# Starting the row maxima ten blocks ahead and the attention four slots earlier

## The chip, the cores and the metric

The kernel runs on one core of one Trainium2 chip. Its engines are TensorE (PE in the profile; its weight loads are PEld), VectorE (DVE), ScalarE (ACT), GpSimd (POOL) and SyncE (SP), which here only issues DMAs. The metric is the device time of one execution in microseconds.

## The reference

One sequence of 2048 tokens of width 512, in float32. Biases, layer norm parameters and a batch do not occur.

```python
xn = layernorm(x)
# attention on layernormed tokens: 32 heads of 16, a window of 256 keys, causal
q, k, v = split(xn @ wqkv)
mask = (i - j >= 0) & (i - j < 256)
s = softmax(where(mask, q @ k.T * 16**-0.5, -1e9)) @ v @ wo
# channel MLP of the normalised tokens, normalised once more, 512 -> 1792 -> 512
g = silu(gelu(layernorm(xn) @ w1 + b1) @ w2 + b2)
out = x + s * g
```

Products are made to float32 precision with three passes of a shorter type: every operand is held as a high part and a low remainder, and high x high, high x low and low x high are summed.

## The kernel before, in words

There are three stages. A prologue normalises x, transposes it into `big` (the array called xnT in the profile, high and low part, four chunks of 512 tokens) and makes the first projections. The attention works on eight quads of four heads in 128 slots (`t` from 0 to 127, sixteen to a quad, one block of 128 keys each). The MLP and the output follow. The change touches the first two.

**Slots.** One loop, `for t in range(-16, end + 1)`, writes out the program in order, and each engine keeps that order; so does SP from the loads on. A slot with t >= 0 does, in this order on PE: `prob_block` for the second half of the heads (scores of one key block against up to 384 queries, into the tile `stb`; ACT takes the exponent to `pt`; POOL blanks the two edge squares), `max_block`, the first half of the slot's fills, `prob_block` for the other half of the heads, the second half of the fills, and `pv_step` for the block before (the product with the values, `zo<-pt,vt`, copied to `oraw`). Negative slots hold fills and, from t = -12, maxima.

**Maxima ahead.** `max_block(n, qb)` for block m = 16 n + qb runs in slot m - `LEAD`, with LEAD = 12: eight score matmuls (into `xy` and `zo`; four in the first two blocks of a quad), then on DVE a predicated copy that masks, and a reduction. After four blocks `max_rows` splits and transposes the maxima on DVE; one slot later SP writes them to DRAM (`mT_d`), and at the end of the slot after that it reads them back as rows of `slots[n % 2]` (the tile `qk`). There they stand as an extra row beside the queries, so that the score matmul subtracts the maximum itself; a matching row of the keys holds ones. A block of scores in slot kb reads queries up to kb + 2.

**The row of ones.** `slots` has two tiles of 128 x 8192. In tile 0 all is cleared at the start by three engines (`clear_rows`). Tile 1 shares its memory with `x23`, the last two chunks of x, and is opened at t = -5; `clear_part` then fills it on ACT in four pieces of 128 x 2048, in slots -4 to -1.

**Fills.** `fills[t, half]` holds matmuls of other work. In the prologue `group(c)` gives four slots per chunk c, from t = 4 c - 16: the Q/K projection of quad 0 (`job_qk(0, c)`, 12 matmuls of 128 x 512), two value jobs (`job_v`, 24 matmuls of 128 x 256 for two blocks of tokens), and the transposes of the next chunk (`job_x`, 16). The projections of quad 1's chunks 0 and 1 (`job_qk(1, 0)` and `(1, 1)`) lie over t = -2 to 2. All other projections are written with `tandem`: two chunks at a time, as matmuls of half the array's height, 48 of them over four to six slots. A projection ends with a copy by ACT (the high part, `sh`), a subtraction that leaves the remainder (`pjr`; by DVE for quad 0, by POOL for the others) and six DMAs into the slot tile: four with the high part, two with the remainder. In `pair_qk` the slot of the POOL subtraction is set by `quiet`, which takes the next free slot whose number leaves 1 or 2 when divided by four.

**PSUM.** `xy`, `zo` and the two banks `fb` are there throughout. Before t = 0 a pool `ps_st` of two more banks serves value jobs and transposes; it closes at t = 0 and its banks become `stb`.

**Layer norm of x.** `lns` says after which slot the last two chunks are normalised: each pair of tiles takes statistics on DVE, a power on POOL, a shift on DVE and the application on ACT.

In the last slots, where no maxima are left, `prob_block` uses `xy` as a second score tile:

```python
both = xy if p and 16 * n + kb + LEAD >= 16 * NQ else stb[0]
```

Of the kernel before, what the change touches and what calls it, by code (L numbers as in the profile page):

```python
# [18 lines left out]
P = 128  # L19
# [4 lines left out]
NQ = H // 4  # L24
EPS = 1e-5
NEG = -3.0e38
LEAD = 12
EARLY = 10


# [19 lines left out]
def mixer_kernel(ctx, tc, x, wqk, wv, wo, w1, b1, w2, b2, out):  # L50
# [96 lines left out]
    def open_slot(i):  # L147
# [9 lines left out]
    w_d = {"w1": dram.tile([P, NF * 512], F32, name="w1_d"), "w2": dram.tile([P, NF * 512], F32, name="w2_d"),  # L157
           "wo": dram.tile([P, 4 * 512], F32, name="wo_d")}
    g_d = dram.tile([NF, P, 512], F32, name="g_d")
    mT_d = dram.tile([NQ, NCH, 32, P], F32, name="mT_d")  # L160


# [10 lines left out]
    def fill_bank():  # L173

        turn[0] ^= 1
        return fb[turn[0]]
# [3 lines left out]
    def clear_rows(i, parts):  # L180

        flat = slots[i].rearrange("p q l t -> p (q l t)")
        ones = upper.unsqueeze(1)
        for eng, lo, hi in parts:
            if eng is nc.scalar:
                eng.copy(flat[:, lo: hi].rearrange("p (k t) -> p k t", t=P), ones.to_broadcast([P, (hi - lo) // P, P]))
            else:
                eng.memset(flat[:, lo: hi].bitcast(F32), float(lo >= 4096))

    def clear_part(k):  # L190
        flat = slots[1].rearrange("p q l t -> p (q l t)")[:, 2048 * k: 2048 * (k + 1)]
        nc.scalar.activation(flat, vt[:, 0, 0, DH: DH + 1].to_broadcast([P, 2048]), AF.Identity, scale=float(k >= 2))

    ident = const.tile([P, P], F32, name="ident")
    upper = const.tile([P, P], F32, name="upper")
    mhalf = const.tile([P, 4], F32, name="mhalf")
# [5 lines left out]
    nc.gpsimd.memset(mhalf, -0.5)  # L202
    make_identity(nc, ident)
    clear_rows(0, ((nc.vector, 0, 2048), (nc.scalar, 4096, 7168), (nc.gpsimd, 2048, 4096), (nc.gpsimd, 7168, 8192)))
    nc.vector.memset(negc, NEG)
    mask = upper.bitcast(I32).unsqueeze(1).unsqueeze(1).to_broadcast([P, 2, 2, P])
    neg = negc.unsqueeze(2).unsqueeze(2).to_broadcast([P, 2, 2, P])
# [106 lines left out]
    def job_v(hf, i):  # L314

        box = []

        def mm(k):
            if k == 0:
                box.append(ps_st.tile([P, 2, 256], F32, tag="b", name=f"pv_{hf}_{i}"))  # L320
            j, kt, (a, b) = k // 12, k % 12 // 3, PASSES[k % 3]
            kb = 2 * i + j
            nc.tensor.matmul(box[0][:, j], big[:, a, kt, P * kb: P * (kb + 1)], wva[:, b, kt],
                             start=(k % 12 == 0), stop=(k % 12 == 11))

        def finish():
            nc.scalar.copy(vt[:, 2 * i: 2 * i + 2, :, 0:DH], box[0].rearrange("p b (h d) -> p b h d", d=DH))
        return [(109, mm, k) for k in range(24)], finish
# [277 lines left out]
    def at(t, fn, *args):  # L606
        plan.setdefault(t, []).append((fn, args))
# [3 lines left out]
    def behind(t, fn, *args):  # L611

        ends.setdefault(t, []).append((fn, args))
# [41 lines left out]
    nc.gpsimd.affine_select(out=upper, in_=upper, pattern=[[1, P]], compare_op=ALU.is_gt,  # L655
                            fill=0.0, base=0, channel_multiplier=-1)
    for i in range(8):
        behind(-14 + i // 4, nc.sync.dma_start, xn_d[i], xs[i // 4][i % 4])

    def group(c):  # L660
        if c == 0:
            (ops, finish), (x_ops, _) = job_v(0, 1), job_x(1)
            return [job_qk(0, 0), job_v(0, 0), (ops[:12] + x_ops, lambda: None), (ops[12:], finish)]
        return [job_qk(0, c), job_v(0, 2 * c), *([job_x(c + 1)] if c + 1 < NCH else []), job_v(0, 2 * c + 1)]
    groups = [(4 * c - 16, 4, group(c)) for c in range(NCH)]
    for t0, n, jobs in groups:
        fills.update(spread(jobs, [(t0 + i // 2, i % 2) for i in range(2 * n)]))

    for place, todo in spread([job_qk(1, 0), job_qk(1, 1)], [(t, k) for t in range(-2, 3) for k in range(2)]).items():
        fills.setdefault(place, []).extend(todo)  # L670
    soon = {}
    tandem(3, 8, pair_qk(1, 2), pair_qk(1, 3))
    for n, spans in enumerate((((9, 14), (15, 19)), ((20, 24), (25, 30)), ((31, 35), (36, 41)), ((42, 47), (48, 53, 51)),
                               ((75, 79), (80, 84)), ((85, 90), (93, 98))), 2):
        for c, span in zip((0, 2), spans):
            tandem(*span[:2], pair_qk(n, c), pair_qk(n, c + 1), *span[2:])
    for i, (t0, t1) in enumerate(((54, 58), (59, 63), (64, 68), (69, 74))):
        tandem(t0, t1, pair_v(2 * i), pair_v(2 * i + 1))
    for f, *span in ((6, 99, 104, 102), (8, 105, 110), (10, 111, 115), (12, 116, 121, 118, 119), (2, 122, 127, 124, 125)):
        tandem(*span[:2], pair_h(f), pair_h(f + 1), *span[2:])  # L680

    for n, t in enumerate((-9, 6, 18, 28, 39, 71, 81), 1):
        at(t - 4, fetch_wqk, n)
        at(t, split_wqk, 0)
        at(t, split_wqk, 1)
# [51 lines left out]
    def pair(l, a):  # L737
        return [l[a][0], l[a + 1][0], l[a][1], l[a + 1][1]]

    ln2, ln3 = (layernorm(xs[c], f"A{c}", True, True) for c in (2, 3))  # L740
    lns = {-16: [ln1[3][1]], -13: pair(ln2, 0) + pair(ln2, 2), -9: pair(ln3, 0), -8: pair(ln3, 2)}

    def fill_in(t, half):
        now[:] = t, half
# [2 lines left out]
            fn(*args)  # L747

    end = 16 * NQ
    for t in range(-16, end + 1):  # L750
        m = t + LEAD
        if t == -5:
            open_slot(1)
            for k in range(4):
                at(-4 + k, clear_part, k)
        if 0 <= t < end:
            if t == 0:
                early.close()
# [465 lines left out]
```

## Time and profile before

| | us |
|---|---|
| median of three runs | 770.96 |
| lowest and highest | 768.57, 771.05 |
| the profiled execution | 770.7 |
| its span, first to last instruction | 769.0 |
| first exponent scores (slot 0 begins) | 71.58 |
| first slot's start to 444.8, where attention ends | 373.22 |
| rest | 324.20 |

The span is what the trace covers; the execution's own time is 1.7 us longer. In the trace all operations are recorded by one helper, so they stand under one line number, and one goes by the tiles' names: `stb<-qk` are the scores, `xy<-qk` and `zo<-qk` the scores of a block of maxima, `pv<-wva,xnT` a value job, `fb<-xnT,wqb` a Q/K projection, `tr<-ident,x` and `fb<-ident,x` transposes. A row of a timeline gives start, length, engine, operation, tiles and shape, and in brackets how long the engine had stood idle before it and what ended that.

### The profile page before, as it was taken

The numbers are of one execution on the slowest core, as the hardware profiler recorded it, in microseconds if no ns is written. First come the engines' busy times: TensorE is split into PE (matmuls) and PEld (weight loads), VectorE is DVE, ScalarE is ACT, GpSimd is POOL, SyncE is SP. The second block draws the span as 40 slices with busy tenths as digits, with TensorE's granted clock in tenths as the row PEclk, the third lists the DMA queues.
The fourth block names the chain that finished last, engine by engine and source line by source line (L and its number), as shares of the span: only waits on it lengthen the run. The fifth ranks groups of instructions, "written<-read, shape, count | busy, mean of one in ns | idle before, by whom it ended". The sixth has DMA issues, their size and how long they took to land.

```text
span 769.0 us, 18778 instructions
## 1 busy us (share of the span) xinstructions
PE 746.9 (97%) x7428; PEld 584.1 (76%) x7428; DVE 533.5 (69%) x865; ACT 435.2 (57%) x724; POOL 280.4 (36%) x567
## 2 busy tenths in 40 slices
PE   9889999999999999999999999999999999999997
PEld 8777666666768887676676678888887888888886
DVE  7886777777777677887875447764657675576473
ACT  6536776767676675777876855444545553342001
POOL 6111666757656554665776800030101100001102
PEclk9989999999999999999999999999999999999999
DMA  7612444645446873454654274641202322243531
GB/s 260 206 44 51 108 106 124 175 114 141 99 103 180 271 225 100 103 156 125 168 156 148 62 267 140 182 160 42 83 20 78 122 73 93 83 155 123 174 96 55
DMA packets 56951, 99.40 MB, mean 129 GB/s; under 512 B 11104, under 2 KB 11360, under 8 KB 56864
## 3 DMA queue, kind: packets, MB, share of 16 engines
q1 hardware_dynamic: 56864, 98.21, 43.9%
q8 instruction: 58, 0.95, 0.5%
q14 instruction: 29, 0.24, 0.1%
HBM read 51.39 MB, written 29.62 MB: 105 GB/s over the span
## 4 chain that ended last, share of the span: by engine, by line
PE 84%; DVE 7%; ACT 4%; issue 2%; POOL 2%; DMA 1%; SPq 0%; DVEq 0%; ACTq 0%
PE acc L42 19%; PE fb L42 17%; PE zo L42 13%; PE p L42 9%; PE stb L42 8%; PE h L42 6%; PE s L42 6%; PE xy L42 5%; ACT pt L42 3%; DVE xy L42 1%; DVE mt L42 1%; PE pv L42 1%; DVE xnT L42 1%; POOL pt L42 1%; DVE bnA L42 1%
## 5 line engine op out<-in xcount | busy, mean ns | idle before, releaser
L42 POOL TENSOR_SCALAR_AFFINE_SELECT pt<-pt 128x256 f32<-128x256 f32 x480 | 193.0, 427 | 159.1 <-ACT pt L42 155.8
L42 ACT ACTIVATE pt<-stb 128x768 f32<-128x768 f32 (+1 forms) x244 | 188.7, 773 | 55.3 <-PE stb L42 46.2
L42 DVE TENSOR_REDUCE mt<-xy 128x4 f32<-128x1024 f32 (+1 forms) x128 | 152.6, 1192 | 4.4
L42 PE MATMUL acc<-w,gh 128*128 128x512 f32 x432 | 133.3, 390 | 0.0
L42 DVE COPY_PREDICATED xy<-upper,zo 128x512 f32<-128x512 int32 x112 | 77.5, 692 | 69.2 <-PE zo L42 67.3
L42 PE MATMUL fb<-xnT,wqb 64*128 64x512 f32 (+1 forms) x684 | 115.2, 405 | 0.5 <-DVE xnT L42 0.5
L42 PE MATMUL zo<-pt,vt 128*17 128x128 f32 x2880 | 103.8, 275 | 2.2 <-DVE xy L42 1.5
L42 PE MATMUL stb<-qk 64*128 64x384 f32 (+1 forms) x488 | 96.6, 392 | 7.1 <-ACT pt L42 5.7
L42 POOL TENSOR_TENSOR xo<-xo,gated 128x512 f32<-128x512 f32 x15 | 20.2, 1347 | 217.8 <-DVE gated L42 194.2
L42 PEld LDWEIGHTS zo<-pt,vt 128*17 128x17 f32 x2880 | 67.4, 97 | 39.4 <-issue 17.8
L42 PEld LDWEIGHTS acc<-w,gh 128*128 128x128 f32 x432 | 80.8, 188 | 16.5
L42 PEld LDWEIGHTS stb<-qk 64*128 64x128 f32 x488 | 45.5, 183 | 52.4 <-ACT pt L42 41.3
L42 PE MATMUL acc<-w,gl 128*128 128x512 f32 x216 | 84.2, 390 | 0.0
L42 PEld LDWEIGHTS fb<-xnT,wqb 64*128 64x128 f32 (+1 forms) x684 | 63.4, 186 | 7.4 <-DVE xnT L42 0.6
L42 PE MATMUL xy<-qk 64*128 64x256 f32 (+2 forms) x536 | 62.0, 305 | 4.9 <-DVE mt L42 4.4
L42 ACT COPY oraw<-zo 128x128 f32<-128x128 f32 x128 | 34.2, 267 | 40.4 <-PE zo L42 36.3
L42 PEld LDWEIGHTS xy<-qk 64*128 64x128 f32 x536 | 44.0, 186 | 16.7 <-DVE mt L42 9.6
L42 PEld LDWEIGHTS acc<-w,gl 128*128 128x128 f32 x216 | 40.5, 188 | 8.8 <-DVE gl L42 0.3
L42 ACT ACTIVATE gated<-acc 128x512 f32<-128x512 f32 x16 | 8.7, 596 | 65.1 <-DVE acc L42 65.1
L42 PE MATMUL s<-wos,ohl 128*128 128x512 f32 (+1 forms) x204 | 44.7, 377 | 0.0
L42 PEld LDWEIGHTS s<-wos,ohl 128*128 128x128 f32 x204 | 36.7, 188 | 7.0
L42 PE MATMUL zo<-qk 64*128 64x128 f32 x448 | 40.7, 259 | 0.0
(182 smaller groups left out, 1159.9 us busy)
## 6 DMA issues: line engine op xcount, KB each, us to landing
qk<-sh SPq DMA_DIRECT2D x128, 128.0 KB
qk<-pjr SPq DMA_DIRECT2D x64, 128.0 KB
oT_d<-oraw SPq DMA_DIRECT2D x32, 256.0 KB
w_d<-in_w_dram SPq DMA_DIRECT2D x14, 512.0 KB
x<-in_x_dram SPq DMA_DIRECT2D x16, 256.0 KB
or<-oT_d SPq DMA_DIRECT2D x16, 256.0 KB
w<-rden_d SPq DMA_DIRECT2D x16, 256.0 KB
xo<-in_x_dram SPq DMA_DIRECT2D x16, 256.0 KB
```

Source lines behind the costliest of these rows:

```text
L42: r = issue(*args, **kwargs)
```

## The change

- `LEAD` becomes 10, and a new `START = -12` is where the loop begins. A block's maxima are made ten slots ahead of its scores, the first of them in slot -10.
- The prologue has three groups of four slots instead of four. The third holds Q/K chunk 2, the transposes of chunk 3, value job 4, Q/K chunk 3 and value job 5. Value jobs 6 and 7 go into slots 2 and 3, and 10 to 12, and use the `fb` banks; quad 1's Q/K chunks 0 and 1 go into slots 0 and 1, and 4 and 5.
- The tandem pairs move: quad 1's second pair from slots 3 to 8 into 6 to 10; quad 2's from 9 to 14 and 15 to 19 into 13 to 17 and 18 to 22; and so on, with five slots for each pair where some had six, until slots 43 to 47. From slot 48 on they stand as before, apart from one start of a second phase (101 in place of 102).
- The weights of quads 1 and 2 are split at slots -4 and 8 (were -9 and 6). The layer norms, the stores of the normalised tokens and the loads move with `START`; relative to the loop's begin, the third chunk's norm comes two slots sooner.
- `clear_part` goes. Of tile 0, once cleared, every fourth partition (32 rows of 32 KB) is copied to DRAM (`rows_d`) by a DMA among the first loads, and at t = 0, where tile 1 is now opened, one DMA copies it into the same partitions of tile 1.

```diff
-LEAD = 12
+LEAD = 10
+START = -12
...
+    rows_d = dram.tile([32, 4 * S], F32, name="rows_d")
...
-    def clear_part(k):
-        flat = slots[1].rearrange("p q l t -> p (q l t)")[:, 2048 * k: 2048 * (k + 1)]
-        nc.scalar.activation(flat, vt[:, 0, 0, DH: DH + 1].to_broadcast([P, 2048]), AF.Identity, scale=float(k >= 2))
...
     clear_rows(0, ((nc.vector, 0, 2048), (nc.scalar, 4096, 7168), (nc.gpsimd, 2048, 4096), (nc.gpsimd, 7168, 8192)))
+    nc.sync.dma_start(rows_d, slots[0][3:P:4].rearrange("p q l t -> p (q l t)").bitcast(F32))
...
-                box.append(ps_st.tile([P, 2, 256], F32, tag="b", name=f"pv_{hf}_{i}"))
+                box.append(ps_st.tile([P, 2, 256], F32, tag="b", name=f"pv_{hf}_{i}") if i < 6 else
+                           fill_bank().rearrange("p (b h) -> p b h", b=2))
...
-        behind(-14 + i // 4, nc.sync.dma_start, xn_d[i], xs[i // 4][i % 4])
+        behind(START + 2 + i // 4, nc.sync.dma_start, xn_d[i], xs[i // 4][i % 4])
...
-        return [job_qk(0, c), job_v(0, 2 * c), *([job_x(c + 1)] if c + 1 < NCH else []), job_v(0, 2 * c + 1)]
-    groups = [(4 * c - 16, 4, group(c)) for c in range(NCH)]
-    for t0, n, jobs in groups:
-        fills.update(spread(jobs, [(t0 + i // 2, i % 2) for i in range(2 * n)]))
-
-    for place, todo in spread([job_qk(1, 0), job_qk(1, 1)], [(t, k) for t in range(-2, 3) for k in range(2)]).items():
-        fills.setdefault(place, []).extend(todo)
+        if c == 1:
+            return [job_qk(0, 1), job_x(2), job_v(0, 2), job_v(0, 3)]
+        return [job_qk(0, 2), job_x(3), job_v(0, 4), job_qk(0, 3), job_v(0, 5)]
+
+    def halves_from(t0, k0, n):
+        return [(t0 + (k0 + i) // 2, (k0 + i) % 2) for i in range(n)]
+
+    for c in range(3):
+        fills.update(spread(group(c), halves_from(START + 4 * c, 0, 8)))
+    for job, places in ((job_qk(1, 0), halves_from(0, 0, 4)), (job_v(0, 6), halves_from(2, 0, 4)),
+                        (job_qk(1, 1), halves_from(4, 0, 4)), (job_v(0, 7), halves_from(10, 1, 5))):
+        for place, todo in spread([job], places).items():
+            fills.setdefault(place, []).extend(todo)
     soon = {}
-    tandem(3, 8, pair_qk(1, 2), pair_qk(1, 3))
-    for n, spans in enumerate((((9, 14), (15, 19)), ((20, 24), (25, 30)), ((31, 35), (36, 41)), ((42, 47), (48, 53, 51)),
+    tandem(6, 10, pair_qk(1, 2), pair_qk(1, 3))
+    for n, spans in enumerate((((13, 17), (18, 22)), ((23, 27), (28, 32)), ((33, 37), (38, 42)), ((43, 47), (48, 53, 51)),
...
-    for n, t in enumerate((-9, 6, 18, 28, 39, 71, 81), 1):
+    for n, t in enumerate((-4, 8, 18, 28, 39, 71, 81), 1):
...
-    lns = {-16: [ln1[3][1]], -13: pair(ln2, 0) + pair(ln2, 2), -9: pair(ln3, 0), -8: pair(ln3, 2)}
+    lns = {START: [ln1[3][1]], -11: pair(ln2, 0) + pair(ln2, 2), -7: pair(ln3, 0), -6: pair(ln3, 2)}
...
-    for t in range(-16, end + 1):
+    for t in range(START, end + 1):
         m = t + LEAD
-        if t == -5:
+        if t == 0:
             open_slot(1)
-            for k in range(4):
-                at(-4 + k, clear_part, k)
+            nc.sync.dma_start(slots[1][3:P:4].rearrange("p q l t -> p (q l t)").bitcast(F32), rows_d)
```

More of the change, by code (lines that the diff above doesn't have):

```diff
@@ L678, in mixer_kernel @@
         tandem(t0, t1, pair_v(2 * i), pair_v(2 * i + 1))
-    for f, *span in ((6, 99, 104, 102), (8, 105, 110), (10, 111, 115), (12, 116, 121, 118, 119), (2, 122, 127, 124, 125)):
+    for f, *span in ((6, 99, 104, 101), (8, 105, 110), (10, 111, 115), (12, 116, 121, 118, 119), (2, 122, 127, 124, 125)):
         tandem(*span[:2], pair_h(f), pair_h(f + 1), *span[2:])
-    for n, t in enumerate((-9, 6, 18, 28, 39, 71, 81), 1):
+    for n, t in enumerate((-4, 8, 18, 28, 39, 71, 81), 1):
         at(t - 4, fetch_wqk, n)
```

## The prediction

> **What bounds the kernel now.** I read the page's totals, then busy time by stretches, then the matrix engine's timeline slot by slot, then the other engines' timelines where it waits.
>
> ```profile
> span 769.0 us, 18778 instructions
> PE 746.9 (97%) x7428; PEld 584.1 (76%) x7428; DVE 533.5 (69%) x865; ACT 435.2 (57%) x724; POOL 280.4 (36%) x567
> ```
>
> ```profile
> 12.00:13.00 1.00, 1.00 (x6) 0.60 (x4) 1.00 (x3) 0.99 (x3) 1.00 (x2) 1.00 1.05 402
> 17.00:18.00 1.00, 1.00 (x11) 1.00 (x9) 0.97 (x4) 0.77 (x1) 0.55 (x1) 1.00 0.00 0
> 30.00:40.00 10.00, 8.55 (x68) 7.23 (x70) 9.72 (x14) 3.77 (x8) 0.00 (x0) 1.00 0.50 145
> 40.00:50.00 10.00, 8.18 (x54) 6.63 (x54) 8.39 (x24) 4.66 (x7) 2.20 (x4) 0.84 0.28 63
> 57.10:71.58 14.48, 14.26 (x105) 11.49 (x104) 9.18 (x13) 9.58 (x8) 0.00 (x0) 1.00 0.25 57
> 71.58:109.82 38.24, 37.07 (x507) 25.28 (x508) 28.61 (x41) 28.01 (x45) 23.23 (x54) 1.00 0.42 100
> 109.82:199.25 89.43, 86.82 (x1284) 61.30 (x1280) 68.60 (x93) 64.06 (x111) 58.47 (x124) 1.00 0.54 132
> 199.25:213.25 14.00, 13.95 (x224) 10.17 (x220) 10.09 (x14) 9.16 (x17) 7.71 (x18) 1.00 0.46 109
> 416.93:422.79 5.86, 5.70 (x80) 3.99 (x81) 1.22 (x4) 3.62 (x6) 3.56 (x10) 1.00 0.77 241
> ```
>
> A window's row gives its length, the busy time of PE, its weight loads, DVE, ACT and POOL, then the clock and the DMA. Attention (71.58 on) is PE's: 37.07 of 38.24, 86.82 of 89.43. The prologue is not: from 30 to 50 us PE has holes and DVE is the busy one (9.72 and 8.39 of 10). Its last four slots (57.10 to 71.58) are PE's again. So work taken from those four slots is no gain in itself: it comes back in attention at PE's rate. Only waits can change the time.
>
> **The change part by part.** It is made against the profiled execution: 770.7 us, span 769.0; the median shown is 770.96.
>
> *A. The prologue.* These rows carry it:
>
> ```profile
> 21.05 1.68 PE L42 MATMUL pv<-wva,xnT 128*128 128x256 f32 x12
> 22.57 2.91 PE L42 MATMUL fb<-xnT,wqb 128*128 128x512 f32 x12
> 25.73 0.44 PE L42 MATMUL xy<-qk 64*128 64x128 f32 x4 [0.25 <-DMA qk<-pjr]
> 45.07 0.51 PE L42 MATMUL xy<-qk 64*128 64x256 f32 x4 [1.54 <-DVE mt L42]
> 60.85 0.51 PE L42 MATMUL xy<-qk 64*128 64x256 f32 x4
> 61.46 3.14 PE L42 MATMUL pv<-wva,xnT 128*128 128x256 f32 x24
> 64.44 0.86 PE L42 MATMUL fb<-xnT,wqb 128*128 128x512 f32 x3
> ```
>
> ```profile
> 19.62 0.69 DVE L42 TENSOR_TENSOR pjr<-xy,sh 128x512 fp32r<-128x512 f32 x1
> 23.05 0.68 DVE L42 BATCH_NORM_STATS2 bnA<-x 128x6 f32<-128x512 f32 x1
> 25.88 0.69 DVE L42 BATCH_NORM_STATS2 bnA<-x 128x6 f32<-128x512 f32 x1
> 28.72 0.75 DVE L42 COPY_PREDICATED_SCALAR xy<-upper,negc 128x512 f32 x1
> 30.16 0.69 DVE L42 TENSOR_TENSOR pjr<-fb,sh 128x512 fp32r<-128x512 f32 x1
> 32.73 1.28 DVE L42 TENSOR_TENSOR xnT<-tr,xnT 128x512 fp32r<-128x512 f32 x2
> 35.12 0.69 DVE L42 COPY_PREDICATED xy<-upper,zo 128x512 f32<-128x512 int32 x1
> 36.98 0.68 DVE L42 TENSOR_TENSOR wqb<-wqkr,wqb 128x512 fp32r<-128x512 f32 x1
> ```
>
> ```profile
> 28.08 1.57 ACT L42 ACTIVATE x<-x,shiftA,rsA 128x512 f32<-128x512 f32 x2 [1.27 <-DVE shiftA L42]
> 22.30 1.50 SPq L42 DMA_DIRECT2D qk<-pjr  x2
> ```
>
> Start to start on PE: a block's eight score matmuls 0.61, a V job 2.98 (24 by 0.124), a chunk's Q/K projection 3.16 (12 by 0.263). On DVE: two tiles of layer norm 2.83, a block of maxima 1.86, a chunk's four remainders 2.39.
>
> Until 21.05 PE's order stays. Then, in the built program, block 0 stands ahead of V job 1's second half and of Q/K chunk 1. It waits for the first projection's rows, which landed at 25.73 (1.93 after the issue's end at 23.80): a 4.7 us hole where V and Q/K ran. DVE now has the third chunk's layer norm (5.67) ahead of chunk 1's remainders, from 20.25; ACT applies the second half 3.77 after that half's start (25.88 to 29.65), so at 26.85, and only then casts chunk 1. DVE's four remainders, half a microsecond behind the first cast, end at 29.7, block 0's maxima at 31.2 (1.44 later). PE holds block 1 for that, and behind block 1 stands Q/K chunk 1: 31.6 to 34.8, nine us later than before. DVE, done with block 1 at 33.7, idles until block 2's scores at 35.4.
>
> The clock was granted at 0.84 in 40 to 50 us, the stretch with a 1.54 us wait. The new holes (4.7, and 27.2 to 31.2) are longer, so I let Q/K chunk 1 run partly at half rate: +1.8 (0 to 3.2, its own length again). [...]
>
> From 31.2 DVE owes, up to block 8: eight blocks 15.0, eight remainders 4.8, layer norm 5.67, two projection remainders 1.3, the weight split 0.7, two transposed sets of maxima 1.1 (an estimate); with 3.6 idle at block 2 and about 1.5 for block 8's rows and latencies, that ends at 64.9. PE meanwhile does Q/K chunk 3 to 66.0; then block 9, V job 5 and its copy (0.61 + 2.98 + 0.7): attention starts at **70.4** instead of 71.58, **-1.2**. Bounds: DVE never idle, 64.0 (-7.6); a second stretch at half clock, 73.5 (+1.9).
>
> *B to E. Attention.* Rows:
>
> ```profile
> 98.60 0.44 PE L42 MATMUL stb<-qk 64*128 64x384 f32 x2 [1.01 <-ACT pt L42]
> 101.40 0.44 PE L42 MATMUL stb<-qk 64*128 64x384 f32 x2
> 115.68 0.33 PE L42 MATMUL stb<-qk 64*128 64x128 f32 x2 [0.22 <-ACT pt L42]
> 118.95 0.44 PE L42 MATMUL stb<-qk 64*128 64x384 f32 x2
> 124.97 0.44 PE L42 MATMUL stb<-qk 64*128 64x384 f32 x2 [0.33 <-ACT pt L42]
> 130.80 0.44 PE L42 MATMUL stb<-qk 64*128 64x384 f32 x2 [0.34 <-ACT pt L42]
> 146.20 0.45 PE L42 MATMUL stb<-qk 64*128 64x384 f32 x2
> 293.70 0.44 PE L42 MATMUL stb<-qk 64*128 64x384 f32 x2 [0.40 <-ACT pt L42]
> 308.59 0.44 PE L42 MATMUL stb<-qk 64*128 64x384 f32 x2
> ```
>
> These are slot starts. A slot with 8 half-height matmuls takes 2.80 (98.60), with 12 it takes 3.27 (115.68): 0.118 each.
> B, slots 0 to 12 (38.24): 48 V matmuls come in (+5.95), ten Q/K matmuls (+2.63), 32 half-height ones go later (-3.76): +4.8 for PE. But slots 0 to 2, whose V products are few, are paced by score, exponent, score, so part is free: I take half, **+2.4** (0.5 to 4.8).
> C, slots 13 to 42 (89.43): six groups of five slots. Slots 15 to 19 took 15.12, slots 20 to 24 15.40: 6 x 15.25 = 91.5, **+2.1** (1.3 to 3.0).
> D, slots 43 to 47 (14.00) become like 75 to 79 (14.89): **+0.9**.
> E, slots 116 and 117 (5.86) keep their maxima, 2 x 3.27: **+0.7** (0 to 1.2).
>
> *F. A new wait at slot 14.* The low half of quad 1's chunk 2 is subtracted on POOL in a slot the helper picks with remainder 1 or 2 by four: slot 9 before, used at 12; now slot 13, used at 14.
>
> ```profile
> 100.76 1.28 POOL L42 TENSOR_TENSOR pjr<-pjr,sh 128x512 fp32r<-128x512 f32 x1
> 102.07 1.18 SPq L42 DMA_DIRECT2D qk<-pjr  x2
> 131.19 0.55 SPq L42 DMA_DIRECT2D qk<-mT_d  x1
> ```
>
> In slot 9 (from 98.60) POOL was done at +3.44 and the two copies' issue ended at +4.65; with A's 1.93 they land at +6.6. Slot 14's block scores, behind its first exponent scores, come some 3.6 after slot 13's start (a slot with 12 fills is 3.27). PE waits **+3.0** (0 if the copies overlap better, 4.5 if SP is late); behind it stand all of slot 14's fills.
>
> *What costs nothing.* The four clears leave ACT, which was busy 9.58 of 14.48 there with PE not waiting for it. The 1 MB copy out stands among the loads: 2.6 us at 402 GB/s, twice that if its 32 long rows go at half the rate, and DMA was empty at 17; the normalised tiles behind it are wanted at 23.1. The copy back, at slot 0, has until slot 6, and the queue's next sends come at slot 2. If that cover fails, those sends slip by up to 5 us, and slot 6 is three slots on. The later weight splits (0.7 DVE) are in the sum; the shifted second phase at 101 moves six matmuls between full slots. The MLP behind attention is unchanged.
>
> Sum: -1.2 + 2.4 + 2.1 + 0.9 + 0.7 + 3.0 = +7.9; 770.7 + 7.9 = **778.6 us**.
>
> **The rivals.** *Faster:* the prologue's waits do not grow. Four slots go (14.48), Q/K chunk 3 and two blocks come (4.4), so attention starts at 61.5: -10.1 + 6.1 = -4.0, **766.7**, if slot 14's wait is hidden too. For it: PE was busy only 8.55 and 8.18 of 10 us in 30 to 50, so there is room for the work that comes in. Against: DVE's chain above ends no earlier than 64.0. It decides if attention starts below 62. 0.15.
> *No change:* DVE stays saturated (64.0) but B to F are paid: -7.6 + 9.1 = +1.5, **772.2**. 0.12.
> *Rows of maxima late:* their DRAM round trip loses two of its four spare slots. Two slots are 5.6 to 6.5 us, the read needs 2.5. Before, one read (131.19) came 6.2 us after its slot's end (124.97); behind 3.1 PE waits. Twice that wait, 6.2: **784.8**. The queue holds less ahead of those reads now, so 0.13.
> The forecast, slower by 4 to 12: 0.60.
>
> **How the numbers follow.** 0.3% (2.3 us) is about what a measurement tells from no change. The faster rival gives 0.15; the no-change case straddles the bound, 0.12; the rest is slower, 0.73. The range leaves out the faster rival's far side and the late rows' far end: 769 to 786; the forecast's own is 774 to 783.
>
> **What would show it.** In the new profile: block 0's scores waiting 4 to 5 us behind chunk 1's transposes; Q/K chunk 1 ending after 34; the first exponent scores near 70; a 3 us wait of PE on the copies of slot 13; five-slot groups of 15.2. Wrong if the first exponent scores start below 64, if slot 14 does not wait, or if PE waits for rows of maxima in many slots.

## The result, and the profile after

The changed kernel takes 795.49 us (median of six runs, 791.43 to 797.5), the kernel before 770.75 in the runs beside it (768.57 to 772.22): a ratio of 1.0321, 95% interval 1.0292 to 1.0351. The forecast was 778.6 us, between 769 and 786: right in its sign, 17 us short in its size. The profiled execution has a span of 794.1 us, 25.1 more than before's 769.0.

First the totals of the page, then busy time by stretches, cut at the same slots as the rows of before (the columns are length, busy time of PE, its weight loads, DVE, ACT and POOL, the clock and the DMA). The last but one row covers slots 48 to 115, and before's row for those slots, which the prediction did not show, stands in the fence behind.

```profile
span 794.1 us, 18775 instructions
PE 753.2 (95%) x7428; PEld 590.5 (74%) x7428; DVE 540.8 (68%) x865; ACT 427.8 (54%) x720; POOL 279.6 (35%) x567
```

```profile
71.31:115.86 44.55, 43.99 (x533) 31.29 (x533) 28.16 (x37) 28.79 (x46) 22.46 (x54) 1.00 0.39 99
115.86:213.69 97.83, 91.37 (x1308) 65.34 (x1305) 70.87 (x95) 64.60 (x113) 58.25 (x123) 0.97 0.53 128
213.69:228.66 14.97, 14.92 (x228) 10.99 (x229) 10.68 (x14) 9.01 (x17) 7.73 (x18) 1.00 0.45 106
228.66:441.42 212.76, 200.20 (x3080) 151.06 (x3080) 165.91 (x226) 145.00 (x250) 127.19 (x277) 0.98 0.53 148
441.42:447.96 6.54, 6.54 (x96) 4.74 (x96) 4.63 (x7) 3.63 (x6) 3.55 (x10) 1.00 0.63 208
```

```profile
213.25:416.93 203.68, 197.42 (x3082) 148.24 (x3081) 160.91 (x226) 145.11 (x250) 126.94 (x277) 1.00 0.54 155
```

Row against row:

| stretch | before | after | difference | forecast |
|---|---|---|---|---|
| prologue, to slot 0 | 71.58 | 71.31 | -0.3 | -1.2 (A) |
| slots 0 to 12 | 38.24 | 44.55 | +6.3 | +2.4 (B) |
| slots 13 to 42 | 89.43 | 97.83 | +8.4 | +5.1 (C 2.1 and F 3.0) |
| slots 43 to 47 | 14.00 | 14.97 | +1.0 | +0.9 (D) |
| slots 48 to 115 | 203.68 | 212.76 | +9.1 | 0 |
| slots 116, 117 | 5.86 | 6.54 | +0.7 | +0.7 (E) |

Two kinds of loss can be told apart in these rows. In slots 0 to 12 PE's busy time itself grew, from 37.07 to 43.99, and it is hardly ever idle: more work, or dearer work. In slots 13 to 42 and 48 to 115 PE's idle time grew as well (6.46 us after against 2.61 before, 12.56 against 6.26), and the clock column fell below 1.00. The waits behind that, from PE's timeline (the brackets give the idle time before the row and what ended it):

```profile
25.50 0.44 PE L43 MATMUL xy<-qk 64*128 64x128 f32 x4 [4.36 <-DMA qk<-pjr]
31.10 0.80 PE L43 MATMUL xy<-qk 64*128 64x256 f32 x4 [2.67 <-DVE mt L43]
31.82 5.22 PE L43 MATMUL fb<-xnT,wqb 128*128 128x512 f32 x12
71.31 0.44 PE L43 MATMUL stb<-qk 64*128 64x384 f32 x2 [0.68 <-ACT vt L43]
123.01 0.80 PE L43 MATMUL xy<-qk 64*128 64x256 f32 x4 [3.52 <-DMA qk<-sh]
285.25 0.44 PE L43 MATMUL stb<-qk 64*128 64x384 f32 x2 [1.97 <-DMA qk<-mT_d]
300.25 0.44 PE L43 MATMUL stb<-qk 64*128 64x384 f32 x2 [1.94 <-DMA qk<-mT_d]
386.50 0.44 PE L43 MATMUL stb<-qk 64*128 64x384 f32 x2 [1.63 <-DMA qk<-mT_d]
```

The first four are the prologue as it was walked in the prediction. The fifth is slot 14. The last three are the starts of slots 66, 70 and 98, where PE waits for rows of maxima: the rival that had been given 0.13. One more wait in slots 48 to 115 is not for rows but for DVE, in slot 82:

```profile
339.73 0.63 PE L43 MATMUL zo<-pt,vt 128*17 128x128 f32 x16 [1.33 <-DVE xy L43]
```

With ten blocks of lead the transposition of four blocks' maxima falls into this slot on DVE, behind a weight split and part of a layer norm and ahead of the masking copy that PE waits for. The wait stands in every trace here with ten blocks of lead throughout, and in none with eleven or twelve.

Busy time by stretches again, over four stretches in which the clock was at half:

```profile
26.37:36.61 10.24, 7.57 (x26) 6.06 (x25) 5.82 (x8) 2.72 (x6) 0.00 (x0) 0.50 0.45 168
121.94:128.77 6.83, 5.76 (x50) 4.29 (x52) 1.92 (x2) 0.86 (x2) 0.41 (x1) 0.50 0.65 162
285.78:289.19 3.41, 3.41 (x40) 3.10 (x41) 1.92 (x2) 1.62 (x2) 0.95 (x3) 0.50 0.77 251
388.18:391.59 3.41, 3.31 (x34) 2.38 (x32) 2.40 (x4) 2.75 (x5) 2.77 (x6) 0.50 0.84 239
```

Each begins during a long wait of the list above or up to 1.7 us behind one (no such stretch follows the wait at 300.25), and each is a multiple of 3.41 us long. So in these traces a wait costs its own length and then up to half of such a stretch: at slot 14 3.52 us and, by the run that took that wait away, 2.72 more.

Why the rows come late is told by the way of four blocks whose rows are needed at slot 66. First the end of their transpose on DVE, after and before:

```profile
272.30 0.21 DVE L43 STREAM_TRANSPOSE mT<-mh 128x32 f32<-128x32 f32 x1
```

```profile
249.70 0.21 DVE L42 STREAM_TRANSPOSE mT<-mh 128x32 f32<-128x32 f32 x1
```

Then SP's timeline, again after and before:

```profile
274.06 1.73 SPq L43 DMA_DIRECT2D qk<-pjr  x2
275.89 0.56 SPq L43 DMA_DIRECT2D mT_d<-mT  x1
276.49 1.78 SPq L43 DMA_DIRECT2D w_d<-in_w_dram  x2
282.57 0.56 SPq L43 DMA_DIRECT2D qk<-mT_d  x1
```

```profile
249.93 0.58 SPq L42 DMA_DIRECT2D mT_d<-mT  x1
258.48 0.56 SPq L42 DMA_DIRECT2D qk<-mT_d  x1
```

After, the rows are ready at 272.51 (the end of the transpose); the write (mT_d<-mT) is issued 3.4 us later, the read (qk<-mT_d) stands 6.1 us behind the end of that issue, and the rows are there at 285.25, 2.1 us after the read's issue. That round trip is 12.7 us, where 10.8 were to be had before the block would have started (283.28). Before, the rows are ready at 249.91 and slot 66 starts at 267.48, 17.6 us on. What holds the read stands in the list of SP's waits, here the row of its own write, not yet landed, for the stretch of the weight copies (after, 255 to 305 us; before, 236 to 290):

```profile
SPq L43 <- DMA mT_d<-mT: 17.6, 4, 6.3
```

```profile
SPq L42 <- DMA mT_d<-mT: 2.6, 1, 2.6
```

The columns are the sum, the number of waits and the longest: 17.6 us in four waits after, one wait of 2.6 before. Reads are held before the weight copies begin at 248.75, too (11.2 us in three waits from 200 to 245 us, after), but not so long that PE waits for them. In its timeline SP keeps the program's order (the copies behind the read of 282.57 went out from 283.18 on), so whatever stands behind a held read is late too, the next write among it: three writes in a row went out 1.0, 3.4 and 5.8 us after their rows were ready.

Slot 98 is another case. Its rows are ready at 374.75 and the write is issued only at 379.76, 5.0 us later, behind copies of projected rows and weights in SP's queue; the read follows 3.3 us behind the end of that issue. There the place in the queue is the largest single part.

### The profile page after: what moved, and what is told of

It reads as the page before. It is cut to its first block, busy times and chain, and to the rows that moved or that the text cites. A ratio compares the mean times of both kernels' runs of the same rounds, so it can differ in the third digit from the quotient of the medians.

```text
span 794.1 us, 18775 instructions
## 1 busy us (share of the span) xinstructions
PE 753.2 (95%) x7428; PEld 590.5 (74%) x7428; DVE 540.8 (68%) x865; ACT 427.8 (54%) x720; POOL 279.6 (35%) x567
## 4 chain that ended last, share of the span: by engine, by line
PE 81%; DVE 7%; ACT 4%; DMA 3%; issue 2%; POOL 2%; SPq 1%; DVEq 0%; ACTq 0%; POOLq 0%
PE acc L43 19%; PE fb L43 18%; PE zo L43 12%; PE p L43 8%; PE stb L43 8%; PE h L43 6%; PE s L43 6%; PE xy L43 4%; ACT pt L43 2%; DVE mt L43 2%; DVE xy L43 1%; DMA qk<-mT_d 1%; DVE xnT L43 1%; POOL pt L43 1%; DVE bnA L43 1%
## 5 line engine op out<-in xcount | busy, mean ns | idle before, releaser
L43 PE MATMUL stb<-qk 64*128 64x384 f32 (+1 forms) x492 | 99.5, 399 | 13.6 <-ACT pt L43 5.9
L43 PEld LDWEIGHTS fb<-xnT,wqb 64*128 64x128 f32 (+1 forms) x684 | 66.5, 191 | 8.0 <-issue 1.0
L43 PEld LDWEIGHTS xy<-qk 64*128 64x128 f32 x532 | 45.7, 188 | 26.2 <-DVE mt L43 11.0
```

The costliest lines, as they stand in the source:

```text
L43: r = issue(*args, **kwargs)
```

## The experiments

### The lead alone

The kernel before with `LEAD` lowered, and nothing else of the change; a few pairs had to begin their second phase in another slot, and one pair ends in slot 25 instead of 24.

```diff
-LEAD = 12
+LEAD = 10
...
-    tandem(3, 8, pair_qk(1, 2), pair_qk(1, 3))
+    tandem(3, 8, pair_qk(1, 2), pair_qk(1, 3), 5)
...
-((20, 24), (25, 30)), ((31, 35), (36, 41))
+((20, 25, 24), (26, 30)), ((31, 35), (36, 41, 40))
...
-(6, 99, 104, 102)
+(6, 99, 104, 101)
```

> The kernel before with one thing of the change alone: maxima ten slots ahead of the attention instead of twelve (the prologue keeps its sixteen slots, the fills their places but for four second phases of a pair, moved by one or two slots). Theory: the shorter lead takes the spare time from the rows of maxima, so the matrix engine waits for their read at the starts of slots 66, 70 and 98 (1.5 to 2 us each, with the clock at half for 3.4 us behind some of them), and slots 48 to 115 take some 212 us instead of 203.7; with slots 116 and 117 (+0.7) and two blocks of scores fewer ahead of the attention (-1.2) that is about 779. Rival: the late rows come from where the fills now stand (five-slot groups, a later slot 55 in time), not from the lead; then slots 48 to 115 stay near 203.7 and the time near 770.

Measured: 784.04 us, ratio 1.0185 (1.0165 to 1.0205). PE waits for the rows at slots 66, 70 and 98, and at 106:

```profile
270.77 0.44 PE L42 MATMUL stb<-qk 64*128 64x384 f32 x2 [1.78 <-DMA qk<-mT_d]
285.38 0.44 PE L42 MATMUL stb<-qk 64*128 64x384 f32 x2 [1.49 <-DMA qk<-mT_d]
372.87 0.44 PE L42 MATMUL stb<-qk 64*128 64x384 f32 x2 [1.17 <-DMA qk<-mT_d]
398.94 0.44 PE L42 MATMUL stb<-qk 64*128 64x384 f32 x2 [1.64 <-DMA qk<-mT_d]
```

The waits came where the theory had them; the time is 5 us above the 779 that it named. Slots 48 to 115 took 214.6 us in its trace (changed kernel 212.8, before 203.7). Of the 25 us that the whole change costs, the two slots of lead alone bring 14.9 (784.04 less 769.19 of the kernel before beside it; 14.2 by the ratio).

With eleven slots (second phases at 7 and 103, and the pair 20 to 24 again drawn out to 25):

> The kernel before with the maxima eleven slots ahead. Theory of the lead: in the changed kernel a read of the rows came 1.6 to 2 us late in three places; one slot more is 2.8 to 3.3 us, so no wait for rows is left, slots 48 to 115 take 203.7, and the time is 770 to 771. Rival: how late a read comes is set by what stands ahead of it in the queue, whatever the lead; then waits of the same 1.5 to 2 us stay in one or more places and the time is 773 or more.

Measured: 773.9 us, 1.0062 (1.0041 to 1.0083). Two waits are left, 2.00 at slot 66 and 1.20 at slot 70, and slots 48 to 115 took 207.7. The expectation of no wait fell: a slot of lead more did not shorten the wait at slot 66 at all. The price falls with the lead, but not by the length of a slot, because the round trip itself grew: from rows ready (252.28) to the start of slot 66 (268.63) it is 16.4 us, where it was 12.7 in the changed kernel. Why it grew was not studied.

### Reading the rows sooner

```diff
-        at(t + 1, nc.sync.dma_start, rows.rearrange("r (i t) -> i r t", i=4), mT)
-        behind(t + 2, nc.sync.dma_start, slots[n % 2][3:P:32, 0, :, 512 * c: 512 * (c + 1)].bitcast(F32),
+        behind(t, nc.sync.dma_start, rows.rearrange("r (i t) -> i r t", i=4), mT)
+        behind(t + 1, nc.sync.dma_start, slots[n % 2][3:P:32, 0, :, 512 * c: 512 * (c + 1)].bitcast(F32),
```

> The changed kernel, with the rows of maxima written to DRAM at the end of their own slot and read back at the end of the next, one slot sooner each. Theory: the three waits for these rows (1.97, 1.94 and 1.63 us) go, and with them the half clock behind two of them; slots 48 to 115 take about 204 instead of 212.8, and the time is 786.5. Rival: the read is held in its queue by the weight copies ahead of it; then sooner issue helps little, one or more of the waits stay, and the time is 791 or more.

Measured: 802.35 us, 1.0403 (1.0366 to 1.044): 7 us slower than the changed kernel. The waits at slots 66 and 70 grew; that at slot 98 went.

```profile
289.82 0.69 PE L43 MATMUL stb<-qk 64*128 64x384 f32 x2 [4.96 <-DMA qk<-mT_d]
306.76 0.44 PE L43 MATMUL stb<-qk 64*128 64x384 f32 x2 [3.80 <-DMA qk<-mT_d]
```

For slots 66 and 70 the first theory (the round trip is simply begun too late) fell with this run, and the rival was too mild; for slot 98 it held. A read placed sooner in the queue still waited for its write to land, and now it held the queue while others could have been issued (SP's waits for these writes sum to 36.0 us from 230 to 320 us, where they were 26.2 in the changed kernel): the write for slot 66 was issued 7.2 us after its rows were ready, that for slot 70 11.2.

### The write on another engine's queue

```diff
-        at(t + 1, nc.sync.dma_start, rows.rearrange("r (i t) -> i r t", i=4), mT)
+        at(t + 1, nc.scalar.dma_start, rows.rearrange("r (i t) -> i r t", i=4), mT)
```

> The changed kernel, with the 32 writes of the rows of maxima issued from ScalarE's queue instead of SP's; the reads stay on SP's. Theory: a round trip needs some 9 us (6 for the write to land beside the weight copies, 2 for the read, two issues) and the shorter lead leaves 11 to 12; what makes it late is the 3.4 to 5.8 us for which the write stands in SP's in-order queue behind other copies and held reads. With the write issued as its rows are ready, the waits at slots 66, 70 and 98 go, slots 48 to 115 take about 204.5 instead of 212.8 and the time is 787. Rival: the read still holds SP's queue until the write has landed, the other copies are late for it, and waits of 1 us or more stay in slots 66 or 70; 792 or more.

Measured: 800.12 us, 1.0383 (1.0357 to 1.0409). In 22 of the 32 round trips the write now goes out within 0.2 us of its rows, where it was 14 in the changed kernel. But SP's reads are held no less: here are their waits in the stretch 230 to 320 us, in this run and in the changed kernel.

```profile
SPq L43 <- DMA mT_d<-mT: 30.3, 6, 8.8
```

```profile
SPq L43 <- DMA mT_d<-mT: 26.2, 7, 6.3
```

The waits at slots 70 and 98 went (0.48 and 0.09 are left), that at slot 66 stayed (1.98). The read for slot 66 was issued at 281.06, hardly sooner than the 282.57 of the changed kernel, and PE started 5.9 us behind the end of its issue, where it was 2.1.

And on ScalarE the issue holds the exponents behind it. Its timeline:

```profile
275.33 0.53 ACTq L43 DMA_DIRECT2D mT_d<-mT  x1
275.91 0.60 ACT L43 ACTIVATE pt<-stb 128x512 f32<-128x512 f32 x1 [2.53 <-DVE mt L43]
```

ScalarE stood idle 2.53 us there, and PE behind it (1.38 us in slot 63). Slots 48 to 115 took 214.7 us, no less than in the changed kernel. So a place at the head of a queue was not enough beside the weight copies: the write (SP was held for one up to 8.8 us) or the read (5.9) was still slow to land.

The same edit in the kernel before with the lead of ten:

> The kernel before with the maxima ten slots ahead and the writes of their rows on ScalarE's queue. Theory: the waits at slots 66, 70, 98 and 106 that the shorter lead brought go, and slots 48 to 115 are back near 204: 784 - 8 = 776. Rival: they stay, 781 or more.

Measured: 786.54 us, 1.0204 (1.0184 to 1.0225). No gain either; waits of 2.79 and 2.49 us at slots 66 and 70, while those at 98 and 106 went.

### Moving the weight copies

One to every fourth slot, in the changed kernel and in the kernel before with the lead of ten:

```diff
-        behind(55 + k, stage_in, kind, j)
+        behind(16 + 4 * k, stage_in, kind, j)
```

> The changed kernel, with the sixteen weight copies of 512 KB to DRAM one to every fourth slot from 16 on (16, 20, ... 76), right behind a read of the rows, where it had one in each of slots 55 to 70. New theory: the read of the rows is held in its in-order queue until its own write has landed, and the write takes 6 us because weight copies are in the transfer queues ahead of it; so the waits at slots 66 and 70 go, slots 48 to 74 take about 80.5 instead of 86.2, and the time is about 789.8. Rival: the round trip is as slow without the copies (the lead alone decides); then the two waits stay and the time is 795.

> The kernel before with the maxima ten slots ahead, as in the first run, and the weight copies one to every fourth slot. Theory: the lead costs what it does in slots 48 to 74 only together with the copies; these slots take 80.4 instead of 86.1 and the time is 778.3. Rival: no gain, 784.

Measured: 798.28 us (1.0373, 1.034 to 1.0406) and 784.31 us (1.02, 1.0177 to 1.0223): no gain in either. In the changed kernel the waits at slots 66 and 70 shrank to 0.84 and 0.97, and one of 3.53 us appeared at slot 34, where there had been none (slots 48 to 74 took 82.9 us instead of 86.2, slots 13 to 42 took 102.9 instead of 97.8):

```profile
190.06 0.44 PE L43 MATMUL stb<-qk 64*128 64x384 f32 x2 [3.53 <-DMA qk<-mT_d]
289.99 0.44 PE L43 MATMUL stb<-qk 64*128 64x384 f32 x2 [0.84 <-DMA qk<-mT_d]
302.60 0.45 PE L43 MATMUL stb<-qk 64*128 64x384 f32 x2 [0.97 <-DMA qk<-mT_d]
```

In the other kernel the wait at slot 70 did not shrink (2.19). So a third test took the copies out of those slots altogether, `behind(71 + k, ...)`:

> The changed kernel with the sixteen weight copies in slots 71 to 86 instead of 55 to 70. Theory: a write of the rows lands late where weight copies are under way, so the waits follow the copies: none at slots 66 and 70, slots 48 to 70 as in the kernel before (65.5 us), and new waits of 1 to 3 us at one or more of slots 74, 82, 86 and 90; the time stays at 795, give or take 3. Rival: the place decides (the second quad slot's sends of these slots); the waits at 66 and 70 stay.

Measured: 794.88 us, 1.0325 (1.0301 to 1.0349). The waits at 66 and 70 are gone, slots 48 to 69 take 66.2 us (before 65.5, changed kernel 71.6), and new waits stand at slots 86 and 90 (that at 98 stays, 1.70):

```profile
347.13 0.52 PE L43 MATMUL stb<-qk 64*128 64x384 f32 x2 [2.48 <-DMA qk<-mT_d]
361.49 0.44 PE L43 MATMUL stb<-qk 64*128 64x384 f32 x2 [1.52 <-DMA qk<-mT_d]
```

The two waits follow the copies: in each of the three places tried for these 8 MB, with this lead, some round trip came late.

### The lead given back in the changed packing

The changed kernel with the subtraction of slot 13 moved to 11 (next section) and two blocks of maxima in each of slots 1 and 2; from slot 3 on they run twelve ahead again.

```diff
-LEAD = 10
+LEAD = 12
...
-        m = t + LEAD
+        ms = [t + 10] if t < 1 else [2 * t + 9, 2 * t + 10] if t < 3 else [t + LEAD]
...
-((13, 17), (18, 22))
+((13, 17), (18, 22, 19))
...
-(6, 99, 104, 101)
+(6, 99, 104, 102)
```

> The changed kernel, with the subtraction of quad 1's chunk 2 in slot 11 and with its lead of twelve blocks given back: slots 1 and 2 do the maxima of two blocks each, and from slot 3 on they run twelve ahead, while the fills keep the changed packing (but for the place of two second phases). Theory: the shorter lead is what uses up the round trip's spare time, so no wait for rows is left in slots 48 to 115, these take about 204.5 instead of some 213, and with two blocks moved from the end to slots 1 and 2 the time is 781.5. Rival: the changed packing makes them late whatever the lead; then waits at 66, 70 or 98 stay and the time is 787 or more.

Measured: 799.45 us, 1.0382 (1.036 to 1.0404): the time was wrong by 18, the mechanism right. Slots 0 to 12 and slots 48 to 115, by stretches:

```profile
71.88:135.25 63.37, 52.42 (x548) 36.55 (x548) 32.89 (x44) 28.88 (x46) 23.53 (x55) 0.87 0.28 74
242.66:446.04 203.38, 197.49 (x3080) 148.19 (x3080) 160.56 (x226) 145.21 (x250) 126.41 (x277) 1.00 0.54 155
```

Slots 48 to 115 are back at 203.4 us (before 203.7), with the changed packing and all copies in place: no wait for rows, clock at 1.00. SP's waits for writes are back to one of 2.6 us (267 to 320 us). The subtraction moved to slot 11 is not what did it: alone (next section) it leaves waits of 1.54, 3.27 and 1.33 us at slots 66, 70 and 98. That settles the +9.1: the lead, not the packing. What the theory left out is where the two extra blocks meet the second quad's projections, which this packing makes just in time for a lead of ten:

```profile
92.23 0.69 PE L43 MATMUL xy<-qk 64*128 64x128 f32 x4 [2.15 <-DMA qk<-pjr]
111.99 0.51 PE L43 MATMUL xy<-qk 64*128 64x256 f32 x4 [3.07 <-DMA qk<-pjr]
129.66 0.80 PE L43 MATMUL xy<-qk 64*128 64x256 f32 x4 [2.69 <-DMA qk<-pjr]
```

Three waits for projected rows, at slots 4, 8 and 12, with half clock behind them, and two of 1.2 us for DVE in the slots with two blocks, make slots 0 to 12 19 us longer than in the changed kernel. The two parts of the change hang together: the late projections force the short lead.

### Slot 14

In the changed kernel, quad 1's chunk 2 has its low half subtracted as soon as it is there:

```diff
-            free = quiet(max(free, t + 1))
+            free = t + 1 if (n, c) == (1, 2) else quiet(max(free, t + 1))
```

> The changed kernel, with the low half of quad 1's chunk 2 subtracted on POOL in slot 11, as soon as it is there, instead of slot 13. Theory: the wait of 3.5 us in slot 14 goes, and with it the stretch of half clock around it; slot 14 takes about 3.0 instead of 9.2, -6.2 us, 789.3. Rival: the half clock is not the wait's doing; then only the 3.5 us go, a stretch at half clock stays near 122 to 129 us, and the time is 792.

Measured: 790.05 us, 1.0258 (1.0218 to 1.0298). Slots 13 to 42 in its trace, by stretches:

```profile
116.26:208.12 91.86, 88.65 (x1309) 63.52 (x1306) 70.81 (x95) 64.54 (x113) 56.96 (x122) 1.00 0.54 133
```

The stretch took 91.86 instead of 97.83. PE's idle time fell by 3.25 us (the wait) and its busy time by 2.72 (the half clock): -6.0, as expected. The bracket of the wait had named copies of a high part (qk<-sh), the ones issued last; but by the semaphore events of the trace the first of these landed only at 123.38, after PE had gone on at 123.01, and the remainder's rows had landed at 122.66. Together with this run that shows that it was the remainder's rows. Slot 14 took 9.23 us in the changed kernel, of which the wait was 3.52.

### The packets of full-height matmuls

The kernel before, with quad 1's chunks 2 and 3 projected as full-height matmuls in slots 3 to 7:

```diff
-    tandem(3, 8, pair_qk(1, 2), pair_qk(1, 3))
+    for place, todo in spread([job_qk(1, 2), job_qk(1, 3)], [(t, k) for t in range(3, 8) for k in range(2)]).items():
+        fills.setdefault(place, []).extend(todo)
```

> The kernel before, with chunks 2 and 3 of quad 1 projected by 24 full-height matmuls over slots 3 to 7, where it had 48 half-height ones over slots 3 to 8. Theory: beside half-height scores a full-height matmul costs 0.30 us instead of the prologue's 0.263, and the scores behind each packet begin 0.1 to 0.15 later; slots 3 to 8 take some 2.7 us more (20.5 instead of 17.85) and the time is 773.5. Rival: the price is the prologue's (24 x 0.263 against 48 x 0.118), +0.65, 771.4; then what slots 0 to 12 of the changed kernel lost beyond the forecast has another cause.

Measured: 772.21 us, 1.0026 (1.0014 to 1.0038): +2.0 us by the ratio, 3.0 between the medians. Slots 3 to 8, in the kernel before and in this one:

```profile
80.75:98.60 17.85, 16.81 (x260) 11.78 (x256) 13.87 (x20) 13.66 (x24) 10.61 (x25) 1.00 0.38 92
```

```profile
79.07:98.89 19.82, 19.12 (x236) 12.23 (x232) 13.04 (x19) 14.54 (x26) 11.91 (x26) 1.00 0.50 123
```

+1.97 us, between theory (2.7) and rival (0.65). Above the prologue's price that is 1.3 us for ten packets, 0.13 each. It seems to lie at the packets' borders; PE's timeline of the changed kernel has one such packet:

```profile
85.93 0.97 PE L43 MATMUL fb<-xnT,wqb 128*128 128x512 f32 x3
86.83 0.44 PE L43 MATMUL stb<-qk 64*128 64x384 f32 x2
```

From 85.93 to 86.83 three matmuls take 0.90, 0.30 each, where twelve in a row in the prologue took 0.263 each. What the 0.13 us a packet is made of, no run here shows.

### The clears, and the prologue

The change's two copies through DRAM, in the kernel before, instead of the four clears:

```diff
-            for k in range(4):
-                at(-4 + k, clear_part, k)
+            nc.sync.dma_start(slots[1][3:P:4].rearrange("p q l t -> p (q l t)").bitcast(F32), rows_d)
```

> The kernel before with the second quad slot's rows cleared by the change's two copies through DRAM instead of the four clears on ScalarE, and nothing else. Theory: both are off the path, 770 to 771. Rival: the copies hold the queue ahead of the projections' rows in the prologue and the attention starts late, by up to 2.6 us (773).

Measured: 769.8 us, 1.0003 (0.9991 to 1.0016): nothing, as said.

In the changed kernel, blocks 0 to 3 behind the second chunk's projection:

```diff
-        if 0 <= m < 4:
-            max_block(0, m)
+        for k in {2: (0, 1), 3: (2, 3)}.get(m, ()):
+            max_block(0, k)
```

> The changed kernel, with blocks 0 to 3 of the maxima moved behind the second chunk's projection (blocks 0 and 1 in slot -8, 2 and 3 in slot -7, instead of one in each of slots -10 to -7). Theory: the two holes of the matrix engine at 21.1 to 25.5 and 28.4 to 31.1 us and the 3.8 us of idle VectorE behind them come from block 0 and 1 standing ahead of that projection; with them behind it, the projection starts at about 27 instead of 31.8 and the attention at about 68.3 instead of 71.3: 792.5. Rival: VectorE's total work sets the start of the attention whatever the order; then it stays within 1 us of 71.3 and the time at 795.

Measured: 797.98 us, 1.0361 (1.0319 to 1.0402). The attention began at 73.51, later than the 71.31 of the changed kernel. The hole did not go, it only changed its cause:

```profile
28.49 5.49 PE L43 MATMUL fb<-xnT,wqb 128*128 128x512 f32 x12 [5.34 <-DVE xnT L43]
```

PE now waits 5.34 us for the second chunk's remainders, which stand on DVE behind the third chunk's layer norm, and the blocks that had filled part of that time come afterwards. So the layer norm was cut in two instead:

```diff
-    lns = {START: [ln1[3][1]], -11: pair(ln2, 0) + pair(ln2, 2), -7: pair(ln3, 0), -6: pair(ln3, 2)}
+    lns = {START: [ln1[3][1]], -11: pair(ln2, 0), -9: pair(ln2, 2), -7: pair(ln3, 0), -6: pair(ln3, 2)}
```

> The changed kernel, with the third chunk's layer norm cut in two: its first two tiles in slot -11, the other two in slot -9 instead of all four in slot -11. Theory: the second chunk's remainders, which stand behind it on VectorE, end 2.8 us sooner, block 1's scores and the second chunk's projection with them (28.5 instead of 31.8), the other half of the layer norm falls into the 3.8 us in which VectorE idled, and the attention starts at 68.1: 792.3. Rival: VectorE is not what sets the start; it stays within 1 us of 71.3, 795.

Measured: 795.43 us, 1.0334 (1.0302 to 1.0366); the profiled execution has a span of 790.6. Its trace is as the theory had it:

```profile
28.34 0.79 PE L43 MATMUL xy<-qk 64*128 64x256 f32 x4
29.07 3.30 PE L43 MATMUL fb<-xnT,wqb 128*128 128x512 f32 x12
67.64 0.44 PE L43 MATMUL stb<-qk 64*128 64x384 f32 x2 [0.68 <-ACT vt L43]
```

Block 1 no longer waits, the projection starts at 29.07 and takes 3.30 instead of 5.22, and the attention starts 3.7 us sooner. That is more than the clock's luck: in the four traces with this edit the attention starts between 67.60 and 68.77, in the nine others with the changed prologue between 70.35 and 73.51. The four timed runs (792.29 to 797.87) do not show it. The same edit on top of the kernel with its lead given back does:

> As the run before, with the third chunk's layer norm cut in two as well. Theory: the attention starts 3 us sooner and 779 is reached; what is then left above the kernel before are the dearer full-height matmuls in slots 0 to 12 and the five-slot groups. Rival: the sooner start brings a wait in slots 0 to 12; 781.5.

Measured: 796.11 us, 1.0342 (1.0316 to 1.0367), against 799.45 in the runs beside it. The attention started at 67.60 instead of 71.88.

### Repairs together

> The changed kernel with both edits, the subtraction in slot 11 and the rows of maxima one slot sooner. Theory: the two losses are independent and add, about -15 us, 780.4; what is left over the kernel before is slots 0 to 12 (+6.3), the five-slot groups (+2), slots 43 to 47 (+1) and the last slots (+0.7). Rival: the clock or another wait takes part of it back; then 783 or more.

Measured: 795.42 us, 1.0326 (1.03 to 1.0352): what the subtraction in slot 11 gave, the sooner reads took, as each did alone.

> The changed kernel with three edits: the low half of quad 1's chunk 2 subtracted in slot 11, the weight copies one to every fourth slot, the third chunk's layer norm cut in two. Theory: the gains add, -6.0 - 5.7 - 3.2 = -14.9, 780.6; above the kernel before then stand the dearer full-height matmuls of slots 0 to 12, the five-slot groups and the wait at slot 98. Rival: some of it is taken back by waits that come next; 784 or more.

Measured: 788.75 us, 1.0248 (1.0226 to 1.027). Slot 14's wait is gone and the attention starts at 68.77, but rows are late at slots 34, 66 and 70 (2.98, 1.39 and 1.87 us).

> The changed kernel with three repairs: the writes of the rows on ScalarE's queue, the low half of quad 1's chunk 2 in slot 11, the third chunk's layer norm cut in two. Theory: the losses add and so do the repairs, -8 - 6 - 3 = -17, 778.5; what is left above the kernel before are the full-height matmuls in slots 0 to 12 (+6.3), the five-slot groups (+2) and slots 43 to 47 and 116 to 117 (+1.7), less an attention that starts 2 to 3 us sooner. Rival: other waits take part back, 782 or more.

Measured: 791.83 us, 1.0271 (1.0241 to 1.0302). The subtraction in slot 11 and the layer norm cut in two hold (slots 13 to 42 take 91.5, the attention starts at 68.63), the writes on ScalarE's queue do not: 3.76 us of wait at slot 70, and slots 48 to 115 take 219.0. No repair of the changed kernel came near the kernel before.

## Why the prediction fell short

**A, the prologue, had the right chain; whether it gains or loses is not settled.** Forecast: a start at 70.4, block 0 held some 4.7 us, block 1 to 31.2, the projection of chunk 1 from 31.6, partly at half clock. In the trace: 71.31, 4.36 us, 31.10, 31.82, half clock from 26.37 to 36.61, which cost that projection 2.1 us (5.22 for 3.16) where 1.8 had been priced. The -1.2 became -0.3 against the one trace that the forecast had; against the start of 69.89 that another execution of the same prologue shows (last section) it would be +1.4. The run with the layer norm cut in two confirms the chain that was named, DVE's layer norm ahead of the remainders.

**B was mis-sized, 2.4 for 6.3.** The step that failed is "part is free: I take half". PE's busy time rose by 6.9 us and its idle time fell only from 1.17 to 0.56, so next to nothing was free to take. The rest is price: the changed kernel has 17 packets of full-height matmuls in slots 0 to 12 where the kernel before had 6, and at the 0.13 us that the run in slots 3 to 8 gave, eleven more are an estimated 1.4 us (it was measured on projections, and part of the 17 are value jobs). The forecast's own 4.8 for PE plus 1.4 makes 6.2 of the 6.3.

**C, D and E were right**: 2.4 (91.86 with slot 14's wait taken away, against 89.43) for 2.1; 1.0 for 0.9; 0.7 for 0.7.

**F had the right wait and half its price.** Forecast 3.0 at slot 14, behind POOL's subtraction in slot 13; the wait was 3.52. The stretch of half clock around it cost 2.7 more, shown by the run that took the wait away (-6.0). The forecast had put a price on the clock in the prologue and put none on it here.

**The step that failed outright is the one that put nothing on slots 48 to 115: +9.1.** The rival with the late rows named the mechanism and sized it at 6.2 for two waits, but got 0.13 on two readings: "the read needs 2.5", and "The queue holds less ahead of those reads now". The second does not bear on these slots, whose fills are as before. What holds a read at slots 66 and 70 is its own write, 6.1 us from landing while weight copies pass, and a held read delays the next write. For the first, to which 0.55 of issue and A's 1.93 add up, the prediction shows no row from beside weight copies. For slot 66 before's trace has 17.6 us between ready rows and the slot, 8.0 of them between write and read and 8.4 behind the read's issue; by the trace's semaphore events the read landed at 264.66, 6.2 us after its issue began and 2.8 before the slot. Two slots, 5.6 to 6.5 us, were to go, so late rows could have been forecast from before's trace.

Shown: the lead alone makes the waits, the lead given back removes them, and those at slots 66 and 70 follow the copies. Not shown: how a write comes to be delayed; no run here looked inside the transfer engines. The wait at slot 98, past the weight copies, is for its largest part the write's 5.0 us in SP's queue: it goes with the lead given back, and also with the sooner reads and with the writes on ScalarE's queue.

So the sum of 7.9 became 25.1: +0.9 in A, +3.9 in B, +0.3 in C, +3.0 in F, +9.1 in the slots that were said not to change.

## What to carry to other kernels

When a lead is shortened, write down for each round trip how long its data lies between ready and needed, subtract what goes, and compare with the longest landing that the trace shows under load, not with the usual one. A wait that goes round a queue issuing in order can grow by itself, because it delays the next one: here three writes in a row went out 1.0, 3.4 and 5.8 us after their rows were ready. Here reading sooner or using another queue cured single waits and made the whole slower; only more lead took them all. Price a wait on the matrix engine at its own length plus up to half of the half-clock stretch that may follow (3.52 and 2.72 us at slot 14), and price matmuls of another height by the packet (here an estimated 0.13 us, from the run in slots 3 to 8).

## What was not expected of the hardware

- Half clock came after short waits. A wait of 1.63 us (slot 98) was followed by a stretch at 0.50, one of 1.94 us (slot 70) was not; in the kernel before with ten slots of lead, one of 1.35 us in slot 82 was, by the length of its matmuls: six half-height ones took 1.59 us from 327.17, where six took 0.92 at 322.33 and 0.91 at 331.36. The stretches in the traces of the kernel before and of the changed kernel, but for those that the end cuts off, are 3.41, 6.83 or 10.24 us long. In the prologue of the kernel before, a wait of 1.54 us was followed by 6.83 us at half clock (46.87 to 53.69); in the run with full-height packets in slots 3 to 7, whose prologue is the same, the same wait of 1.54 by 3.41 us (46.23 to 49.64), and the attention started at 69.89 instead of 71.58: 1.7 us between two executions of the same code. Against that start the changed prologue is not 0.3 us better but 1.4 worse.
- A write of 16 KB took 6.1 us from the end of its issue until the read behind it was let go, with weight copies of 512 KB about, and SP was held up to 8.8 us for one that was issued from ScalarE. Weight copies are not the only thing that slows it: in the changed kernel a write before any weight copy (issued at 212.35) held its read for 5.0 us from the end of its issue. Why was not studied.
- A full-height packet of three matmuls between half-height ones takes 0.90 us, against 0.79 for three of a long row.
